# A fused attention and MLP layer on one core: semaphore waits that keep GpSimd's additions and some VectorE operations apart, three open rounds of sums, and a new written-out order

## The chip, the core and the metric

The kernel runs on one core of one Trainium2 chip. The core has a matrix engine (TensorE, PE in the profile), three engines for element-wise work (VectorE or DVE, ScalarE or ACT, GpSimd or POOL), a synchronization engine (SyncE, SP) and DMA queues that SP and GpSimd issue to. Each engine works through its own instruction stream in order and waits on semaphores where it needs another's result. The metric is the device time of one execution in microseconds. Three runs of the kernel before took 199.99 to 200.40, with a median of 200.25.

## The reference

One sequence of S = 2048 rows with D = 448 features in bf16. Two residual blocks follow each other, each behind a layer norm without weights:

```python
h  = x + A(layernorm(x)) ;  h2 = h + B(layernorm(h))

# A: 16 heads of 28; each position attends to itself and to 7 earlier ones, 2 apart
qkv = x @ wqkv
logits[s, w] = q[s] . k[s - 2*w] / sqrt(28)     for w = 0..7, masked where s - 2*w < 0
o = softmax_w(logits) @ v[s - 2*w] ;  return o @ wo

# B: a mixer and an MLP, F = 1792
h  = gelu(layernorm(x) @ w1)                    # 448 x 448
hs = concat(quarters of h, shifted by 1, -1, 2, -2 rows) @ w2
x1 = x + hs
return x1 + gelu(layernorm(x1) @ w3) @ w4       # 448 x 1792, 1792 x 448
```

## The kernel before

The rows are worked on in four tiles of 512 (t = 0 to 3), in 16 blocks of 128 partitions each. The phases of a tile are:

- `phase_N1`: statistics of the rows and the normalization `lntm`, then `doubled`, a small copy of the last 64 columns beside the others, so that pairs of matmuls can use half the rows each; `transposed` makes the transposed tile `actT`, either on TensorE (with the identity `ident`) or with a transposing DMA of the SP queue.
- `phase_A1` and `phase_V`: projections to queries, keys and values. ScalarE (and for some groups VectorE) takes the sums out of PSUM; for the values into `vt`, from where DMAs of GpSimd's queue put overlapping windows of 80 rows into `vw`.
- `phase_A2`: VectorE multiplies each query with its eight keys, `qk_r`, in four products per tile (128 x 4096, the last 128 x 2048); TensorE sums them over the heads' columns with the constant `zc`. Then the softmax: the largest logit `mx`, the difference `ls`, the exponential on ScalarE, the sum `zs`, its reciprocal, and the weights `pb`, all on VectorE but the exponential. TensorE transposes `pb`, ScalarE stores it in the `arena`.
- `phase_A3`: VectorE spreads the weights into a block diagonal `bd_r` (80 x 2048, four per tile), TensorE multiplies it with `vw`, ScalarE takes the result out as `actT`, TensorE multiplies with `wo_s` and adds the residual.
- `phase_B1`: the second layer norm and the matmuls with `w1`; ScalarE applies the GELU.
- `phase_B2`, `phase_W3`, `phase_B3`: these run on five units of 3, 4, 4, 4 and 1 blocks, since the row shifts of the mixer cross the tiles' borders. `phase_B2` multiplies with `w2_s` (the matmuls `w_s`, `arena`), VectorE adds the scaled residual (one `scalar_tensor_tensor` per block, `arena<-xin,rs_y,ps`), then comes a third layer norm. GpSimd adds the residual once more, in place: 16 additions `xb += xin` (`arena<-arena,xin`), one per block. `phase_W3` is the matmul with `w3` and its GELU into `h3T`, `phase_B3` the matmul with `w4`; VectorE scales and adds (`ost`), and SP's queue stores the result.

A layer norm's variance goes through VectorE (`rs_x`), then either GpSimd (`rs_y`, a power of -1/2) or ScalarE; `nm` is the negated mean. So at the places that matter the same stretch has VectorE's `rs_x`, `nm`, normalizations (`lntm`) and softmax beside GpSimd's power and additions.

The order is not made by a scheduler at run time. The phases first record operations with their tiles, readers and writers (`_Sched.group`). `schedule` then walks through `ORDER`, a written-out list of 1096 operation numbers, and hands each operation to its engine's stream in that order. On the way it gives out buffers (pools of PSUM banks, tiles of `lntm`, `actT`, `qk_r`, `bd_r` and others) and works out a modelled time for each operation, from which it derives some dependences between DMAs, the number of filler matmuls, and the order in which waits are listed. `_emit_plan` turns every dependence between two streams into a semaphore wait, unless an earlier wait implies it. So the modelled times change little but the order in the list changes each engine's stream. An operation flagged `block` is one that the model takes to run either on VectorE or on GpSimd at a time: the GpSimd additions on one side, and on the other the `qk_r` and `bd_r` products and most normalizations of VectorE. Before the change this is only a rule for the modelled times:

```python
if op.eng == "pool":
    waiting = op if blocked > st else None
    st = entry = max(st, blocked)
    if op.block: held = st + dur
elif op.block:
    ...                        # a waiting GpSimd operation is set back
    else: st = max(st, held)
    blocked = st + dur
```

The tile pool `P_win` has no memory behind it. `contract`, which makes the matmul groups of a projection, holds one of its tiles for each round of up to four groups: with one tile a second round cannot open in the list before the first has closed.

Nearly every instruction of the profile bears line 1090, `inst = getattr(eng, meth)(**kw)` in `emit_engine`, so instructions are told apart by their tiles.

Of the kernel before, what the change touches and what calls it, by code (L numbers as in the profile page):

```python
# [6 lines left out]
ALU = mybir.AluOpType  # L7
# [181 lines left out]
class _Sched:  # L189
# [69 lines left out]
    def schedule(self, dma_bw=240.0, dma_fixed=2000.0, table_load=1300.0):  # L259
# [18 lines left out]
        blocked = held = entry = 0.0; waiting = None  # L278
        assert sorted(ORDER) == list(range(n))
        for idx in ORDER:  # L280
# [45 lines left out]
            else:  # L326
# [3 lines left out]
                if op.eng == "pool":  # L330
                    waiting = op if blocked > st else None
                    st = entry = max(st, blocked)
                    if op.block:
                        held = st + dur
                elif op.block:
                    if waiting is not None and st <= entry + 50.0:
                        late = st + dur - entry
                        free["pool"] += late; waiting.t1 += late; entry += late
                        for ch in children[waiting.idx]:
                            if waiting in ch.deps:  # L340
                                rdy[ch.idx] = max(rdy[ch.idx], waiting.t1 - (self.OWN if ch.eng == "pool" else 0.0))
                        if waiting.block:
                            held += late
                    else:
                        st = max(st, held)
                    blocked = st + dur
# [67 lines left out]
def bass_sequential_preLN__sliding_local_dilated__mixer_s_mlp__prompt_kernel(  # L414
# [17 lines left out]
    EPS = 1e-5  # L432
# [15 lines left out]
    with ExitStack() as es:  # L448
# [41 lines left out]
        P_win = _Pool("win", None, 1)  # L490
# [39 lines left out]
        def dma(chan, out_ap, in_ap, nbytes, dur=450.0, eng="sp", behind=(), **kw):  # L530
            op = S.add(eng, "dma_start", dur, 1000.0 if eng == "pool" else 0.0 if not callable(chan) else -1300.0, chan=chan, nbytes=nbytes, out=out_ap, in_=in_ap, **kw)
            op.odeps.update(behind)
            return op
# [598 lines left out]
```

## Time and profile before

| | before |
|---|---|
| median of three runs | 200.25 us (199.99 to 200.40) |
| the profiled execution | 199.96 us |
| its span | 198.2 us |
| TensorE busy | 189.7 us, 96%, 1667 matmuls |
| VectorE busy | 121.7 us, 61%, 222 instructions |
| ScalarE busy | 143.4 us, 72%, 321 instructions |
| GpSimd busy | 46.0 us, 23%, 96 instructions |
| granted TensorE clock | 1.0 |

The profile shows one execution of the program, taken by the hardware's profiler. The span runs from its first to its last instruction. The slices cut the span into 40 equal parts of 4.95 us, and each digit is an engine's busy share in tenths (9 is 90% or more). The chain of waits follows the work that ended last back from the end: start, length, engine and instruction. A row of a timeline is a run of like instructions on one engine: the start (us), the length, engine, line, operation, tiles written and read, shape, count; a bracket at its end is the idle time just before it and what ended that. Rows can overlap by the depth of an engine's pipeline.

### The profile page before, as it was taken

What the parts mean: (1) busy time and instruction counts of PE and PEld (TensorE: products, weight loads), DVE (VectorE), ACT (ScalarE), POOL (GpSimd) and SP (SyncE); (2) the same over time, 40 slices, a digit from 0 to 9 for tenths busy, and PEclk for the clock granted to TensorE, in tenths of its full rate; (3) what the DMA queues carried; (4) which work ended last, traced back from release to release, by engine and by line L of the source; (5) the groups of instructions that cost most, each with busy time, mean ns of one, the idle gap of its engine ahead of it and who ended that gap; (6) DMA issues with size and microseconds to landing.
All of it is one profiled execution on the core that took longest, in us unless ns stands there. A gap on an engine that the chain in (4) does not pass through costs nothing.

```text
span 198.2 us, 4119 instructions
## 1 busy us (share of the span) xinstructions
PE 189.7 (96%) x1667; PEld 92.6 (47%) x1667; DVE 121.7 (61%) x222; ACT 143.4 (72%) x321; POOL 46.0 (23%) x96
## 2 busy tenths in 40 slices
PE   6899999889999989999989999999999999999994
PEld 2555333443454545544545444455444455446753
DVE  5888889999989999947957775101314052310024
ACT  4849986997999999997589699991345961645300
POOL 6540199003500000036040204302050000760000
PEclk9999999999999999999999999999999999999999
DMA  5950579943995000055410410009300023210003
GB/s 160 326 162 3 107 179 224 189 88 58 237 286 198 5 3 3 10 107 126 86 20 0 80 31 3 23 0 202 102 26 0 2 40 66 73 46 0 3 0 116
DMA packets 24467, 16.81 MB, mean 85 GB/s; under 512 B 17824, under 2 KB 22880, under 8 KB 24448
## 3 DMA queue, kind: packets, MB, share of 16 engines
q1 hardware_dynamic: 22368, 9.24, 19.7%
q0 software_dynamic: 2080, 7.31, 14.8%
q8 instruction: 13, 0.21, 0.4%
q14 instruction: 6, 0.05, 0.1%
HBM read 7.91 MB, written 1.84 MB: 49 GB/s over the span
## 4 chain that ended last, share of the span: by engine, by line
PE 62%; ACT 19%; DVE 8%; DMA 5%; POOL 4%; issue 1%; SPq 0%
PE ps L1090 62%; ACT arena L1090 5%; ACT actT L1090 5%; ACT vt L1090 3%; DMA vw<-vt 3%; ACT lntm L1090 2%; DVE qk_r L1090 2%; DMA xin<-in_A_x_dram 1%; DVE lntm L1090 1%; POOL w_s L1090 1%; POOL vw L1090 1%; DVE arena L1090 1%; ACT xin L1090 1%; POOL wo_s L1090 1%; ACT L1085 1%
## 5 line engine op out<-in xcount | busy, mean ns | idle before, releaser
L1090 PE MATMUL ps<-actT,arena 128*128 128x512 bf16 (+6 forms) x404 | 71.5, 344 | 0.3 <-ACT actT L1090 0.2
L1090 PEld LDWEIGHTS ps<-actT,arena 128*128 128x128 bf16 (+1 forms) x404 | 30.7, 97 | 37.4 <-issue 6.7
L1090 PE MATMUL ps<-arena,h3T 128*128 128x448 bf16 (+1 forms) x238 | 46.4, 342 | 0.0
L1090 ACT ACTIVATE h3T<-ps 128x512 bf16<-128x512 f32 (+1 forms) x60 | 30.6, 578 | 14.0 <-PE ps L1090 13.8
L1090 ACT ACTIVATE arena<-ps 128x512 bf16<-128x512 f32 (+5 forms) x64 | 32.0, 524 | 12.0 <-PE ps L1090 11.5
L1090 DVE SCALAR_TENSOR_TENSOR ost<-ps,mrs,arena 128x448 bf16<-128x448 f32 (+1 forms) x17 | 10.9, 654 | 37.8 <-PE ps L1090 35.7
L1090 DVE TENSOR_TENSOR qk_r<-arena 128x4096 bf16<-128x4096 bf16 (+1 forms) x16 | 31.8, 2016 | 2.8 <-PE ps L1090 2.8
L1090 PEld LDWEIGHTS ps<-arena,h3T 128*128 128x128 bf16 x238 | 22.6, 98 | 19.3 <-issue 0.5
L1090 POOL DMA_DIRECT2D vw<-vt x15 | 9.0, 605 | 48.9 <-DMA actT<-lntm 48.4
L1090 DVE TENSOR_TENSOR bd_r<-arena,bmask 80x2048 bf16<-80x2048 bf16 x16 | 18.7, 1214 | 2.2 <-ACT arena L1090 2.2
L1090 POOL TENSOR_TENSOR arena<-arena,xin 128x448 f32<-128x448 f32 x16 | 16.3, 1037 | 15.2 <-ACT lntm L1090 14.5
L1090 ACT ACTIVATE actT<-ps 128x512 bf16<-128x512 f32 (+2 forms) x27 | 17.8, 679 | 2.6 <-PE ps L1090 2.4
L1090 ACT ACTIVATE lntm<-arena,nm 128x448 bf16<-128x448 f32 x16 | 10.6, 662 | 8.6 <-DVE nm L1090 8.6
L1090 POOL TENSOR_TENSOR rs_y<-rs_x,mhalf 128x4 f32<-128x4 f32 (+1 forms) x5 | 4.7, 934 | 50.1 <-DVE rs_x L1090 50.1
L1090 PE MATMUL ps<-wo_s,actT 128*128 128x448 bf16 x64 | 14.5, 354 | 1.7 <-ACT actT L1090 1.6
L1090 DVE BATCH_NORM_STATS2 st<-xin 128x6 f32<-128x448 bf16 x24 | 13.8, 610 | 1.7 <-DMA xin<-in_A_x_dram 1.6
L1090 PE MATMUL ps<-actT,w_s 128*112 128x512 bf16 (+1 forms) x64 | 14.5, 387 | 0.0
L1090 DVE SCALAR_TENSOR_TENSOR arena<-xin,rs_y,ps 128x448 f32<-128x448 bf16 x16 | 10.4, 677 | 6.7 <-PE ps L1090 6.6
L1090 PE MATMUL ps<-w_s,arena 112*128 112x448 bf16 x64 | 13.6, 352 | 0.3 <-ACT arena L1090 0.3
L1090 PE MATMUL ps<-arena,actT 128*128 128x448 bf16 (+1 forms) x64 | 12.3, 353 | 0.5 <-ACT arena L1090 0.5
L1090 PEld LDWEIGHTS ps<-actT,w_s 128*112 128x112 bf16 (+1 forms) x64 | 6.5, 128 | 6.1 <-issue 2.0
L1090 PEld LDWEIGHTS ps<-w_s,arena 112*128 112x128 bf16 x64 | 6.0, 98 | 6.3 <-ACT arena L1090 1.1
(73 smaller groups left out, 190.4 us busy)
## 6 DMA issues: line engine op xcount, KB each, us to landing
out_dram<-ost SPq DMA_DIRECT2D x15, 112.0 KB, 1.7
arena<-in_B_w_dram POOLq DMA_DIRECT2D x1, 1568.0 KB, 15.2
arena<-in_B_w_dram POOLq DMA_DIRECT2D x1, 1344.0 KB, 10.4
vw<-vt POOLq DMA_DIRECT2D x4, 320.0 KB, 5.3
vw<-vt POOLq DMA_DIRECT2D x4, 256.0 KB, 5.2
xin<-in_A_x_dram SPq DMA_DIRECT2D x2, 448.0 KB, 5.8
xin<-in_A_x_dram SPq DMA_DIRECT2D x3, 224.0 KB, 5.0
arena<-in_A_wqkv_dram SPq DMA_DIRECT2D x1, 672.0 KB, 4.8
```

The lines of the kernel that those rows point to most:

```text
L1085: eng.preload_act_table_set("natural_log_exp_and_others")
L1090: inst = getattr(eng, meth)(**kw)
```

## The change

It has four parts. First, in `schedule` the flag `block` becomes a real wait: each flagged GpSimd operation now depends on the last flagged VectorE operation ahead of it in the list, and each flagged VectorE operation on the last flagged GpSimd one. Second, more of VectorE's operations get the flag: the small `nm` and `rs_x` operations and the `doubled` copies. Third, the pool `P_win` has three tiles instead of one. Fourth, two constants of the modelled DMA times are changed, and `ORDER` is another permutation of the same 1096 numbers.

```diff
 ORDER = [
-    0, 9, 8, 10, 1, 2, 3, 11, 6, 4, 35, 22, 36, 5, 37, 12, 23, 38, 13, 24, 14, 25, 39, 15, 26, 46, 16, 40, 27, 52, 17, 28, 41, 18, 53, 29, 47, 60,
...
+    0, 9, 10, 1, 2, 3, 11, 4, 35, 22, 36, 37, 12, 23, 38, 13, 24, 14, 25, 39, 15, 26, 46, 16, 40, 27, 17, 47, 28, 52, 41, 48, 18, 29, 53, 19, 30, 66,
...
-    def schedule(self, dma_bw=240.0, dma_fixed=2000.0, table_load=1300.0):
+    def schedule(self, dma_bw=215.0, dma_fixed=2000.0, table_load=1300.0):
...
-        blocked = held = entry = 0.0; waiting = None
+        blocked = entry = 0.0; waiting = None; guard = dict(dve=None, pool=None)
...
                 if op.eng == "pool":
-                    waiting = op if blocked > st else None
-                    st = entry = max(st, blocked)
                     if op.block:
-                        held = st + dur
+                        waiting = None
+                        if guard["dve"]:
+                            op.deps.add(guard["dve"]); st = max(st, guard["dve"].t1)
+                        guard["pool"] = op
+                    else:
+                        waiting = op if blocked > st else None
+                        st = entry = max(st, blocked)
                 elif op.block:
+                    if guard["pool"]:
+                        op.deps.add(guard["pool"]); st = max(st, guard["pool"].t1)
+                    guard["dve"] = op
                     if waiting is not None and st <= entry + 50.0:
...
-                        if waiting.block:
-                            held += late
-                    else:
-                        st = max(st, held)
                     blocked = st + dur
...
-        P_win = _Pool("win", None, 1)
+        P_win = _Pool("win", None, 3)
...
-            op = S.add(eng, "dma_start", dur, 1000.0 if eng == "pool" else ...
+            op = S.add(eng, "dma_start", dur + 100.0 * (eng == "pool"), 1000.0 if eng == "pool" else ...
...
-            dve("tensor_scalar", 4, ns=78.0, out=nm[:, kind, lo:lo + m], ...
+            dve("tensor_scalar", 4, ns=78.0, block=True, out=nm[:, kind, lo:lo + m], ...
...
-                dve("tensor_scalar", 4, ns=78.0, out=rs_x[:, kind, 0, i:i + m], in0=var, scalar1=by, scalar2=EPS, op0=ALU.mult, op1=ALU.add)
+                dve("tensor_scalar", 4, ns=78.0, block=True, out=rs_x[:, kind, 0, i:i + m], in0=var, scalar1=by, scalar2=EPS, op0=ALU.mult, op1=ALU.add)
...
-            dve("tensor_copy", 64, ns=142.0, out=ln(lambda v: v[:, lo:lo + n, D:512]), ...
+            dve("tensor_copy", 64, ns=142.0, block=True, out=ln(lambda v: v[:, lo:lo + n, D:512]), ...
```

The flagged `tensor_scalar` operations shown stand for all of them: every `nm` and every `rs_x` operation of VectorE has the flag after the change. The program has the same operations on the same engines: 1668 matmuls instead of 1667, one more of the filler matmuls that TensorE runs while it waits for the first tile.

More of the change, by code (lines that the diff above doesn't have):

```diff
@@ L530, in dma @@
         def dma(chan, out_ap, in_ap, nbytes, dur=450.0, eng="sp", behind=(), **kw):
-            op = S.add(eng, "dma_start", dur, 1000.0 if eng == "pool" else 0.0 if not callable(chan) else -1300.0, chan=chan, nbytes=nbytes, out=out_ap, in_=in_ap, **kw)
+            op = S.add(eng, "dma_start", dur + 100.0 * (eng == "pool"), 1000.0 if eng == "pool" else 0.0 if not callable(chan) else -1300.0, chan=chan, nbytes=nbytes, out=out_ap, in_=in_ap, **kw)
             op.odeps.update(behind)
@@ L596, in sums_stats @@
             lo, m = tiles[0], len(tiles)
-            dve("tensor_scalar", 4, ns=78.0, out=nm[:, kind, lo:lo + m], in0=mv[:, kind, lo:lo + m, 0], scalar1=-1.0 / D, scalar2=None, op0=ALU.mult)
+            dve("tensor_scalar", 4, ns=78.0, block=True, out=nm[:, kind, lo:lo + m], in0=mv[:, kind, lo:lo + m, 0], scalar1=-1.0 / D, scalar2=None, op0=ALU.mult)
             for n, i in enumerate(tiles):
@@ L619, in rstd @@
                 if not summed and (norm == "a" or kind == 1):
-                    dve("tensor_scalar", 4, ns=78.0, out=nm[:, kind, i:i + m], in0=mv[:, kind, i:i + m, 0], scalar1=-1.0, scalar2=None, op0=ALU.mult)
+                    dve("tensor_scalar", 4, ns=78.0, block=True, out=nm[:, kind, i:i + m], in0=mv[:, kind, i:i + m, 0], scalar1=-1.0, scalar2=None, op0=ALU.mult)
                 power_act(first)
@@ L629, in rstd @@
             if not summed and (norm == "a" or kind == 1):
-                dve("tensor_scalar", 4, ns=78.0, out=nm[:, kind, i:i + m], in0=mv[:, kind, i:i + m, 0], scalar1=-1.0, scalar2=None, op0=ALU.mult)
+                dve("tensor_scalar", 4, ns=78.0, block=True, out=nm[:, kind, i:i + m], in0=mv[:, kind, i:i + m, 0], scalar1=-1.0, scalar2=None, op0=ALU.mult)
             if kind == 1:
-                dve("tensor_scalar", 4, ns=78.0, out=rs_x[:, kind, 1, i:i + m], in0=var, scalar1=by * (1.0 + EPS), scalar2=EPS * EPS,
+                dve("tensor_scalar", 4, ns=78.0, block=True, out=rs_x[:, kind, 1, i:i + m], in0=var, scalar1=by * (1.0 + EPS), scalar2=EPS * EPS,
                     op0=ALU.mult, op1=ALU.add)
@@ L635, in rstd @@
             elif summed:
-                dve("tensor_scalar", 4, ns=78.0, out=rs_x[:, kind, 0, i:i + m], in0=var, scalar1=by, scalar2=EPS, op0=ALU.mult, op1=ALU.add)
+                dve("tensor_scalar", 4, ns=78.0, block=True, out=rs_x[:, kind, 0, i:i + m], in0=var, scalar1=by, scalar2=EPS, op0=ALU.mult, op1=ALU.add)
             else:
-                dve("tensor_scalar", 4, ns=78.0, out=rs_x[:, kind, 0, i:i + m], in0=var, scalar1=EPS, scalar2=None, op0=ALU.add)
+                dve("tensor_scalar", 4, ns=78.0, block=True, out=rs_x[:, kind, 0, i:i + m], in0=var, scalar1=EPS, scalar2=None, op0=ALU.add)
             if kind == 1:
@@ L641, in rstd @@
                     shifts(1)
-                dve("tensor_scalar", 4, ns=78.0, out=rs_x[:, kind, 0, i:i + m], in0=var, scalar1=by, scalar2=EPS, op0=ALU.mult, op1=ALU.add)
+                dve("tensor_scalar", 4, ns=78.0, block=True, out=rs_x[:, kind, 0, i:i + m], in0=var, scalar1=by, scalar2=EPS, op0=ALU.mult, op1=ALU.add)
             power(0)
@@ L674, in doubled @@
         def doubled(ln, lo, n):
-            dve("tensor_copy", 64, ns=142.0, out=ln(lambda v: v[:, lo:lo + n, D:512]), in_=ln(lambda v: v[:, lo:lo + n, 384:D]))
+            dve("tensor_copy", 64, ns=142.0, block=True, out=ln(lambda v: v[:, lo:lo + n, D:512]), in_=ln(lambda v: v[:, lo:lo + n, 384:D]))
         def transposed(ln, how, n=4, w=2):
```

74 rows, old and new, of the table ORDER are left out of this document.

## The prediction

> **What bounds the kernel now.** I read the page's totals and slices first, then the chain of waits, then the timeline of each engine around every wait of TensorE.
>
> ```profile
> span 198.2 us, 4119 instructions
> PE 189.7 (96%) x1667; PEld 92.6 (47%) x1667; DVE 121.7 (61%) x222; ACT 143.4 (72%) x321; POOL 46.0 (23%) x96
> ...
> PE   6899999889999989999989999999999999999994
> ...
> DVE  5888889999989999947957775101314052310024
> ACT  4849986997999999997589699991345961645300
> ```
>
> The reader is to see two halves. In slices 7 to 17 (35 to 85 us) VectorE and ScalarE are at 9 tenths beside TensorE; from slice 21 on TensorE alone is full. The chain says the same:
>
> ```profile
> 87.94 3.43 DVE qk_r L1090 x2
> ...
> 92.62 1.11 DVE lntm L1090
> 93.73 0.91 DVE nm L1090
> ...
> 101.71 93.95 PE ps L1090 x664
> ```
>
> From 101.71 us to the end TensorE runs 664 matmuls without a wait. Nothing that another engine does there pays, unless it makes TensorE wait. So a gain has to come from TensorE's idle time before 101.71, which the timeline of TensorE gives:
>
> ```profile
> 6.77 0.40 PE L1090 MATMUL ps<-ident,lntm 128*128 128x128 bf16 x4 [0.70 <-DVE lntm L1090]
> ...
> 37.34 1.79 PE L1090 MATMUL ps<-arena,actT 64*128 64x448 bf16 x10 [0.52 <-ACT arena L1090]
> ...
> 41.63 0.93 PE L1090 MATMUL ps<-wo_s,actT 128*128 128x448 bf16 x4 [0.86 <-ACT actT L1090]
> ...
> 44.75 0.93 PE L1090 MATMUL ps<-wo_s,actT 128*128 128x448 bf16 x4 [0.26 <-ACT actT L1090]
> ...
> 64.49 2.44 PE L1090 MATMUL ps<-w_s,arena 112*128 112x448 bf16 x12 [0.34 <-ACT arena L1090]
> ...
> 73.97 0.93 PE L1090 MATMUL ps<-wo_s,actT 128*128 128x448 bf16 x4 [0.45 <-ACT actT L1090]
> ...
> 78.65 4.50 PE L1090 MATMUL ps<-actT,arena 128*128 128x384 bf16 x28 [0.20 <-ACT actT L1090]
> ...
> 91.81 1.05 PE L1090 MATMUL ps<-qk_r,zc 128*32 128x512 bf16 x16
> ...
> 97.54 3.38 PE L1090 MATMUL ps<-arena,h3T 128*128 128x448 bf16 x17
> 101.71 0.64 PE L1090 MATMUL ps<-ident,pb 128*80 128x128 bf16 x8 [0.79 <-DVE pb L1090]
> ```
>
> Six waits on ScalarE between 37 and 79 us make 0.52 + 0.86 + 0.26 + 0.34 + 0.45 + 0.20 = 2.63 us, and one on VectorE at 101.71 makes 0.79 us. All of them together are 3.42 us, the most that a new order can win.
>
> **The wait at 101.71, where the change acts.** The timelines of GpSimd and VectorE show what made `pb` late:
>
> ```profile
> 91.53 1.05 POOL L1090 TENSOR_TENSOR rs_y<-rs_x,mhalf 128x4 f32<-128x4 f32 x1 [1.80 <-DVE rs_x L1090]
> 92.57 2.05 POOL L1090 TENSOR_TENSOR arena<-arena,xin 128x448 f32<-128x448 f32 x2
> ...
> 91.28 0.16 DVE L1090 TENSOR_SCALAR rs_x<-mv 128x4 f32<-128x4 f32 x1
> 92.62 1.11 DVE L1090 TENSOR_SCALAR lntm<-xin,nm,rs_y 128x448 bf16<-128x448 bf16 x1 [1.17 <-POOL rs_y L1090]
> 93.65 0.99 DVE L1090 TENSOR_SCALAR nm<-mv 128x4 f32<-128x4 f32 x1
> 94.56 1.00 DVE L1090 TENSOR_SCALAR lntm<-xin,nm,rs_y 128x448 bf16<-128x448 bf16 x3
> 95.60 0.23 DVE L1090 COPY lntm<-lntm 128x256 bf16<-128x256 bf16 x1
> 95.74 0.68 DVE L1090 TENSOR_REDUCE mx<-ps 128x64 f32<-128x512 f32 x1
> 96.46 0.69 DVE L1090 TENSOR_TENSOR ls<-ps,mx 128x512 f32<-128x512 f32 x1
> 97.06 0.67 DVE L1090 SCALAR_TENSOR_TENSOR arena<-xin,rs_y,ps 128x448 f32<-128x448 bf16 x1
> ...
> 100.96 0.69 DVE L1090 TENSOR_TENSOR pb<-ls,zs 128x512 bf16<-128x512 f32 x1
> ...
> 103.97 1.25 DVE L1090 TENSOR_TENSOR bd_r<-arena,bmask 80x2048 bf16<-80x2048 bf16 x1 [2.24 <-ACT arena L1090]
> ```
>
> While the two additions run (92.57 to 94.62) VectorE gets through two instructions. Three normalizations behind them take 1.00, 0.33 each, so from 92.62 to 94.56 about 1.5 us are lost to the additions.
>
> [...]
>
> In the changed program, the built order on each engine is: on GpSimd one addition, then the power `rs_y`, both after `rs_x`; on VectorE `rs_x`, `mx`, `nm` (waits for that addition), `ls`, four normalizations, the copy, then the four residual operations, `zs`, the reciprocal and `pb`. By rows: `rs_x` ends at 91.44; the addition (half of 2.05) ends about 92.5, the power (1.05) about 93.6. `mx` needs the 16 sums that end at 91.81 + 1.05 = 92.86, so it runs from 92.9, `nm` finds its addition done, and `ls` starts about 93.7 and lets go at 94.3 (0.60, from 96.46 to 97.06). The power is done by then. Four normalizations are 1.33, the copy 0.14: 95.8. From the first residual operation to the end of `pb` it is 101.65 - 97.06 = 4.59, with the same operations in between, so `pb` ends at 100.4 instead of 101.65. TensorE's last matmul before it ends at 97.54 + 3.38 = 100.92. The 0.79 goes whole, with 0.5 us to spare. Bounds: from 0 to -0.79; I take -0.79, since the margin is worked out from rows of this very stretch.
>
> What is late next: VectorE's `bd_r` products now wait for GpSimd's 46th update, the power and two additions after the next `rs_x`, which is put just ahead of `pb` (about 99.7): 99.7 + 1.05 + 2.05 = 102.8. They started at 103.97 and had waited 2.24 for ScalarE, so 1.2 us of cover are left; without it, the first TensorE reader of `bd_r` is several microseconds further on. The other guard waits (for `ost`, `nm`, the last copy) lie in the part where TensorE runs without a break; I cost them at nothing, bar the last, which is a rival below.
>
> **The new order before 90 us.** These are its parts on VectorE and ScalarE:
>
> ```profile
> 1.06 0.81 DVE L1090 MEMSET wo_s<- 128x896 uint32 x1 [1.06 <-PEq L1117]
> 1.87 0.27 DVE L1090 MEMSET vt<- 128x256 uint32 x1
> ...
> 8.23 1.15 DVE L1090 BATCH_NORM_STATS2 st<-xin 128x6 f32<-128x448 bf16 x2 [0.51 <-DMA xin<-in_A_x_dram]
> ...
> 87.94 3.43 DVE L1090 TENSOR_TENSOR qk_r<-arena 128x4096 bf16<-128x4096 bf16 x2 [2.47 <-PE ps L1090]
> ...
> L1090 ACT ACTIVATE vt<-ps 128x448 bf16<-128x448 f32 x16 | 8.4, 552 | 0.0
> ```
>
> The first copy stands one normalization later (0.33 by the row above), and TensorE waits for it at 6.77. Cost 0 to +0.33; I take 0, because TensorE meets ScalarE again at 37.34 with 0.52 idle. One extra filler matmul falls into the idle 0.70 before 6.77: nothing.
>
> Two memsets, 0.81 + 0.27 = 1.08, move from the start, where VectorE waited for the first load, to behind the first four tiles. There VectorE was idle 0.51 for a load, so it comes up to 0.57 later into its full stretch. The third query product also waits for sums that TensorE now issues behind three more matmuls, up to 0.6 (0.2 each, 3.38 for 17 in the row at 97.54). Cost to TensorE 0 to +1.2; I take 0: VectorE stands idle 2.47 at 87.94, waiting for TensorE, which covers a VectorE that is late by itself.
>
> The last value projection's evictions are moved ahead of the first GELU's table load: one more of 0.55 before the `w_s` matmuls of 64.49, and one fewer before those of 73.97. Three of the matmuls of another tile stand between the `bd_r` ones ahead of 41.63, whose wait of 0.86 they can fill. Bounds for all six waits on ScalarE: from -2.63 to +0.55. I take 0, nearest to what both full engines allow: what TensorE saves at 41.63, it finds again as a VectorE or ScalarE that is not ready at the next place.
>
> GpSimd's queue issues the `vw` and weight loads in another sequence, but the same ones, and the transposing load at 40 us no longer waits for the `vw` load that stood last. No bracket in TensorE's timeline names those loads before 90 us: 0. The planner's constants (bandwidth, GpSimd's issue) and the three `win` tiles do nothing on the chip except through the order.
>
> Sum: -0.79 + 0 + 0 = -0.8 us. The profiled execution took 199.96 for a span of 198.19; it becomes 199.2. It lies 0.29 under the median of 200.25, so the median becomes 199.4.
>
> **The rivals.**
>
> *The order wins more.* If half of the 2.63 us of waits on ScalarE go as well, 200.25 - 0.79 - 1.3 = 198.2. For it: the matmuls put ahead of 41.63, and rounds of sums that may interleave. Against: the 9s of ScalarE and VectorE in slices 7 to 17.
>
> *The wait comes back.* The `w_s` matmuls behind 101.71 need the transposing load of the tile whose copy ended at 95.83.
>
> ```profile
> actT<-lntm SPq DMA_TRANSPOSE x8, 4.4
> ```
>
> That copy stays where it is (95.8), the load lands 4.4 later at 100.2, and TensorE would come for it at 101.4. If the load takes 1.2 us more, or `pb` loses the 0.5 of its margin and more, TensorE stands again, for up to 0.79: 199.4 to 200.25, and taken at 200.1, since a load that misses its time by more than its cover mostly gives the whole stall back. Against: the cover of 1.2.
>
> *Slower: VectorE's full stretch starts later and TensorE follows.* The place is 8 to 79 us. Price: 0.57 + 0.6 = 1.2 on VectorE, and 0.55 on ScalarE ahead of the GELU. If TensorE's start of W3 (78.65) is later by more than 1.2, the 0.79 no longer pays for it and the kernel is slower by over 0.4; with the whole price, 200.25 - 0.79 + 1.75 = 201.2, and with the first copy's 0.33 on top 201.5. For it: slices 7 to 17 have hardly a gap. Against: the idle 2.47 and the idle of 2.63.
>
> A smaller danger sits in the tail:
>
> ```profile
> 170.21 0.18 DVE L1090 COPY lntm<-lntm 128x64 bf16<-128x64 bf16 x1
> ...
> 177.31 0.39 PE L1090 MATMUL ps<-ident,lntm 128*128 128x128 bf16 x4
> ```
>
> The copy for the last tile ended 6.9 us before TensorE came for it; now it waits for three additions (3.1, at 2.05 for two) and sits behind `ost` operations. By the additions alone 3.8 are left, so I cost it at nothing; if that cover is gone, TensorE stands there by what is missing, and this belongs to the slower share.
>
> **How the numbers follow.** The forecast 0.42 (199.4, its own range 198.8 to 199.8); the order wins more 0.10 (198.2); the wait comes back 0.15 (200.1); slower 0.33 (200.7 to 201.5). 0.2% is 0.4 us, about what a measurement of this kernel can tell from no change. Faster is the first two, 0.52; same 0.15; slower 0.33. The range reaches over all four: 198.1 to 201.5.
>
> **What would show it.** Right: TensorE's row for `pb` carries no bracket; VectorE's normalizations behind the power take 0.4 each; `nm` takes 0.17; W3 starts within 0.5 us of 78.65. Wrong: brackets between 37 and 79 us that sum to more than 3.4; a VectorE with slices under 8 tenths between 35 and 85; a new bracket behind 101 us that names VectorE or GpSimd.

## The result, and the profile after

The changed kernel takes 199.41 us in the median of 22 runs (198.42 to 201.59), the kernel before 200.01 in 22 runs beside it (199.67 to 201.60). The ratio is 0.9967, with a 95% interval of 0.9952 to 0.9982. The forecast was 199.4. Here and below the ratios and their intervals are taken over the undisturbed executions and are no quotients of the medians, which are taken over all, so the two can differ by some 0.2%.

The profiled execution took 199.71 us for a span of 197.9. Its totals and slices, from the page:

```profile
span 197.9 us, 4122 instructions
PE 190.2 (96%) x1668; PEld 93.4 (47%) x1668; DVE 120.2 (61%) x222; ACT 143.3 (72%) x321; POOL 48.0 (24%) x96
...
PE   6999999879999889999999999999999999999994
...
DVE  3998989998999999767946777000343043230024
```

Counted from 0, TensorE's slice 20 (99 to 104 us) was an 8 and is a 9; slice 8 (40 to 45 us) was an 8 and is a 7. VectorE's slice 16 (79 to 84 us) was a 9 and is a 7. The timelines of VectorE and GpSimd around `pb` in the changed kernel:

```profile
88.63 3.43 DVE L1093 TENSOR_TENSOR qk_r<-arena 128x4096 bf16<-128x4096 bf16 x2 [1.74 <-PE ps L1093]
92.00 0.17 DVE L1093 TENSOR_SCALAR rs_x<-mv 128x4 f32<-128x4 f32 x1
93.42 0.69 DVE L1093 TENSOR_REDUCE mx<-ps 128x64 f32<-128x512 f32 x1 [1.25 <-PE ps L1093]
94.03 0.16 DVE L1093 TENSOR_SCALAR nm<-mv 128x4 f32<-128x4 f32 x1
...
94.75 1.31 DVE L1093 TENSOR_SCALAR lntm<-xin,nm,rs_y 128x448 bf16<-128x448 bf16 x4
...
100.14 0.69 DVE L1093 TENSOR_TENSOR pb<-ls,zs 128x512 bf16<-128x512 f32 x1
103.73 3.49 DVE L1093 TENSOR_TENSOR bd_r<-arena,bmask 80x2048 bf16<-80x2048 bf16 x3 [2.90 <-POOL arena L1093]
```

```profile
92.25 1.04 POOL L1093 TENSOR_TENSOR arena<-arena,xin 128x448 f32<-128x448 f32 x1 [1.27 <-DVE rs_x L1093]
93.25 1.05 POOL L1093 TENSOR_TENSOR rs_y<-rs_x,mhalf 128x4 f32<-128x4 f32 x1
100.22 1.49 POOL L1093 TENSOR_TENSOR rs_y<-rs_x,mhalf 128x4 f32<-128x4 f32 x1 [5.92 <-DVE rs_x L1093]
101.69 2.01 POOL L1093 TENSOR_TENSOR arena<-arena,xin 128x448 f32<-128x448 f32 x2
```

The addition now runs while VectorE waits for TensorE's sums anyway; four normalizations take 1.31, 0.33 each, and `nm` 0.16. TensorE's timeline on the same stretch and its waits before 80 us:

```profile
37.59 1.23 PE L1093 MATMUL ps<-arena,actT 64*128 64x448 bf16 x7 [0.67 <-ACT arena L1093]
40.01 0.42 PE L1093 MATMUL ps<-bd_r,vw 80*32 80x64 bf16 x32 [0.22 <-issue]
...
42.41 0.93 PE L1093 MATMUL ps<-wo_s,actT 128*128 128x448 bf16 x4 [0.86 <-ACT actT L1093]
...
65.08 1.69 PE L1093 MATMUL ps<-w_s,arena 112*128 112x448 bf16 x8 [0.62 <-ACT arena L1093]
69.86 0.42 PE L1093 MATMUL ps<-ident,pb 128*80 128x128 bf16 x4 [0.19 <-ACT actT L1093]
71.88 0.93 PE L1093 MATMUL ps<-wo_s,actT 128*128 128x448 bf16 x4 [0.44 <-ACT actT L1093]
75.03 0.93 PE L1093 MATMUL ps<-wo_s,actT 128*128 128x448 bf16 x4 [0.45 <-ACT actT L1093]
...
92.32 1.05 PE L1093 MATMUL ps<-qk_r,zc 128*32 128x512 bf16 x16
...
98.20 3.38 PE L1093 MATMUL ps<-arena,h3T 128*128 128x448 bf16 x17
101.42 0.61 PE L1093 MATMUL ps<-ident,pb 128*80 128x128 bf16 x8
```

`pb` has no bracket. But the last sums of products start at 92.32 where they started at 91.81, so in this execution TensorE comes 0.51 later to the stretch, and the waits between 37 and 80 us sum to 3.45 where they summed to 2.63. From here on one measure is useful: TensorE's own work from the start of these sums to `pb` is 101.42 - 92.32 = 9.10 us. VectorE's way from the same start to the end of `pb` was 101.65 - 91.81 = 9.84 before and is 100.83 - 92.32 = 8.51. So the stretch went from 0.74 too long to 0.59 of margin. TensorE's start on `pb` moved from 9.90 to 9.10 behind the start of the sums, and 0.8 us are won there; in this execution 0.51 of it had been lost ahead.

### The profile page after: what moved, and what is told of

The parts are those of the page before. It is cut to its first block, busy times and chain, and to the rows that moved or that the text cites. A ratio compares the mean times of both kernels' runs of the same rounds, so it can differ in the third digit from the quotient of the medians.

```text
span 197.9 us, 4122 instructions
## 1 busy us (share of the span) xinstructions
PE 190.2 (96%) x1668; PEld 93.4 (47%) x1668; DVE 120.2 (61%) x222; ACT 143.3 (72%) x321; POOL 48.0 (24%) x96
## 4 chain that ended last, share of the span: by engine, by line
PE 68%; ACT 21%; POOL 4%; DMA 3%; issue 1%; DVE 1%; POOLq 0%; ACTq 0%
PE ps L1093 68%; ACT arena L1093 6%; ACT lntm L1093 4%; ACT vt L1093 4%; DMA vw<-vt 3%; ACT actT L1093 3%; POOL vw L1093 2%; POOL w_s L1093 1%; POOL wo_s L1093 1%; ACT xin L1093 1%; ACT L1088 1%; ACT L1093 1%; ACT ls L1093 1%; ACT nmr L1093 0%; ACT rs_x L1093 0%
## 5 line engine op out<-in xcount | busy, mean ns | idle before, releaser
L1093 PE MATMUL ps<-actT,arena 128*128 128x512 bf16 (+6 forms) x404 | 72.7, 344 | 0.0
L1093 PE MATMUL ps<-arena,h3T 128*128 128x448 bf16 (+1 forms) x238 | 48.0, 342 | 0.0
L1093 ACT ACTIVATE arena<-ps 128x512 bf16<-128x512 f32 (+4 forms) x64 | 31.5, 526 | 9.8 <-PE ps L1093 9.0
L1093 PE MATMUL ps<-arena,actT 128*128 128x448 bf16 (+1 forms) x64 | 12.8, 354 | 0.7 <-ACT arena L1093 0.7
L1093 DVE COPY lntm<-lntm 128x256 bf16<-128x256 bf16 (+2 forms) x16 | 3.3, 208 | 14.5 <-ACT lntm L1093 12.4
L1093 ACT ACTIVATE vt<-ps 128x448 bf16<-128x448 f32 x16 | 8.4, 554 | 1.8 <-DMA vw<-vt 1.8
```

## The experiments

OLD and NEW are the two lists. Where a kernel mixes them, the list is cut behind operation 550, VectorE's last query product (88 to 92 us); the two parts ahead of it differ by two operations on either side. Each line of times has the kernel before from the same chip beside it.

**The new list behind the cut alone.**

```diff
-ORDER = NEW
+ORDER = OLD[:OLD.index(550) + 1] + [x for x in NEW if x not in OLD[:OLD.index(550) + 1]]
```

> The changed kernel with the list of before up to VectorE's last query product (88 to 92 us), and the new list, with its waits, behind it. Theory 'two parts': the new list behind the cut is worth the stall of 0.79 us at pb and the new list ahead of it costs some 0.5 (in the two profiles TensorE comes 0.50 us later to the last sums of products, 92.32 against 91.81, and starts on pb 0.29 earlier, 101.42 against 101.71). Then this kernel is at 200.0 - 0.8 to 0.95 = 199.05 to 199.2, below the changed kernel's 199.4. Theory 'late part only': the new list ahead of the cut costs nothing in the median, and the 0.5 is one execution's: then it is at 199.4, as the changed kernel. pb's row on TensorE carries no bracket in both.

Measured: 199.30 us (12 runs), before 200.09; ratio 0.9968 (0.9945 to 0.9991). `pb` has no bracket; from the sums to its end it is 100.32 - 91.81 = 8.51. The late part alone is the gain, 0.8 in the medians. The median lies between the forecasts of the two theories; the ratio is that of the whole change (0.9967), which speaks for "late part only", but with an interval of 0.2% to either side the times alone don't decide it.

**The new list ahead of the cut alone,** the list of before behind it, without the added waits (both `op.deps.add(guard[...])` taken out, as in the next experiment).

```diff
-ORDER = NEW
+ORDER = NEW[:NEW.index(550) + 1] + [x for x in OLD if x not in NEW[:NEW.index(550) + 1]]
```

> The reverse: the new list up to VectorE's last query product, the list of before behind it, without the added waits. Theory 'two parts': 200.0 + 0.5 = 200.5 or, since a later TensorE waits less for pb, 200.0 to 200.5, with pb's bracket between 0.3 and 0.8. Theory 'late part only': 200.0, with a bracket of 0.8.

Measured: 199.86 us (12 runs), before 200.09; ratio 0.9995 (0.9976 to 1.0014): no difference. From the sums to the end of `pb` it is 101.45 - 91.60 = 9.85 as before. The bracket of 0.8 isn't there by name, since the planner put four filler matmuls into the gap it saw; TensorE still starts on `pb` only at 101.51.

**The new list throughout, without the added waits.**

```diff
                         if guard["dve"]:
-                            op.deps.add(guard["dve"]); st = max(st, guard["dve"].t1)
+                            st = max(st, guard["dve"].t1)
...
                     if guard["pool"]:
-                        op.deps.add(guard["pool"]); st = max(st, guard["pool"].t1)
+                        st = max(st, guard["pool"].t1)
```

> The changed kernel without the added waits: same list, same instructions on each engine in the same sequence, but the GpSimd additions no longer wait for VectorE nor VectorE for them. Theory 'the order does it': the first addition starts some 1.2 us sooner, at 91.0, beside the query product, and pb keeps its 0.5 us of margin: 199.4, within 0.2. Rival 'the waits do it': the addition and the query product hold each other up by up to the length of the addition (1.04 us), the last sums come that much later, and pb is late by up to 0.8: 199.7 to 200.2, with a product behind 88 us that takes over 2.2 us instead of 2.06 mean.

Measured: 200.32 us (12 runs), before 200.09; ratio 0.9998 (0.9978 to 1.0019). The gain is gone. The timelines of GpSimd, VectorE and TensorE show where:

```profile
90.99 1.02 POOL L1093 TENSOR_TENSOR arena<-arena,xin 128x448 f32<-128x448 f32 x1
```

```profile
88.68 4.42 DVE L1093 TENSOR_TENSOR qk_r<-arena 128x4096 bf16<-128x4096 bf16 x2 [1.74 <-PE ps L1093]
```

```profile
93.15 1.05 PE L1093 MATMUL ps<-qk_r,zc 128*32 128x512 bf16 x16 [0.72 <-DVE qk_r L1093]
```

The addition starts 1.26 us sooner, at 90.99, and the two query products take 4.42 instead of 3.43: 0.99 more, for an addition of 1.02. The way from the sums to `pb` is 8.52, as good as with the waits, but the sums start 0.72 late. The rival "the waits do it" holds here, with the very product that it named; the median lies 0.1 above its range.

**The waits, flags and open rounds with the list of before.**

```diff
-ORDER = NEW
+ORDER = OLD
```

> The changed kernel with the list of before throughout: the added waits, the flags and the three open rounds alone. In the list the two additions stand behind normalizations, so that by the waits VectorE runs four normalizations at 0.33 first, and the copy waits for one addition, the next nm for the second. Theory 'the order does it': the waits move the lost time from the normalizations to the copy and to nm, and pb stays late: 199.8 to 200.2, pb's bracket 0.5 to 0.9. Rival 'the waits do it': pb's bracket under 0.3, 199.3 to 199.6.

Measured: 199.96 us (12 runs), before 200.09; ratio 0.9996 (0.9977 to 1.0015): no difference. Its profile is that of its slowest execution, 201.59 us, so only the distances within the stretch are read from it. The timelines of VectorE, GpSimd and TensorE:

```profile
94.76 1.00 DVE L1093 TENSOR_SCALAR lntm<-xin,nm,rs_y 128x448 bf16<-128x448 bf16 x3
96.91 0.23 DVE L1093 COPY lntm<-lntm 128x256 bf16<-128x256 bf16 x1 [1.15 <-POOL arena L1093]
```

```profile
95.84 1.03 POOL L1093 TENSOR_TENSOR arena<-arena,xin 128x448 f32<-128x448 f32 x1 [1.50 <-DVE lntm L1093]
```

```profile
93.58 1.05 PE L1093 MATMUL ps<-qk_r,zc 128*32 128x512 bf16 x16
...
102.52 1.03 PE L1093 MATMUL ps<-ident 128*128 128x512 bf16 x4
103.38 0.61 PE L1093 MATMUL ps<-ident,pb 128*80 128x128 bf16 x8
```

The normalizations are quick (0.40 for the first, 1.00 for the other three), and the copy then waits 1.15 us for the addition. From the sums to the end of `pb` it is 102.97 - 93.58 = 9.39: 0.45 less than before, but TensorE is through with its own work 8.94 behind the start of the sums. Here too the planner has put four fillers into the gap, from 102.52 to 103.38, so that TensorE starts on `pb` only 0.41 after its end, where it took 0.06 before. So waits alone put the copy's wait of 1.15 in the place of the longer normalizations and take off a part of the delay, and in this kernel the fillers use most of that part up (TensorE starts on `pb` 9.80 behind the start of the sums, before 9.90). What the waits alone would gain without these fillers, no run shows; an estimate from these rows is 0.4 us at most. As built, they gain nothing without the new list, and the new list gains nothing without them.

**Two additions moved, in the kernel before.** No added wait; operations 416 and 418 are taken out of OLD and put behind 529, the next power.

```diff
-    ..., 527, ..., 416, ..., 418, ..., 529, ..., 417, ...
+    ..., 527, ..., 529, 416, 418, ..., 417, ...
```

> The kernel before, with its own list and no added wait; only the two GpSimd additions of 92.57 to 94.62 are moved behind the next power (to about 102.8, ahead of the third). Theory 'those two additions make pb late': the normalization and nm behind the power take 0.36 and 0.17 again instead of 1.11 and 0.99, pb ends some 1.6 us earlier at about 100.1, TensorE's row for pb (which comes at 100.9) has no bracket of 0.79: 200.05 - 0.8 = 199.25. Rival 'something else that the new list moves does it' (the power behind one addition, the sums ahead of the normalizations): the bracket stays above 0.5 and the time within 0.3 of 200.05. A third outcome is that the bracket goes and the time stays, because three additions now run beside the bd_r products at 103 to 106.

Measured: 199.16 us (10 runs, 198.76 to 199.35), before 200.01; ratio 0.9947 (0.9927 to 0.9967). Moving two operations of 1096 gives the whole gain of the change (0.9967); the intervals don't tell the two apart. The timelines of VectorE, GpSimd and TensorE:

```profile
92.98 0.40 DVE L1090 TENSOR_SCALAR lntm<-xin,nm,rs_y 128x448 bf16<-128x448 bf16 x1 [1.18 <-POOL rs_y L1090]
93.29 0.16 DVE L1090 TENSOR_SCALAR nm<-mv 128x4 f32<-128x4 f32 x1
...
103.21 5.04 DVE L1090 TENSOR_TENSOR bd_r<-arena,bmask 80x2048 bf16<-80x2048 bf16 x3 [2.24 <-ACT arena L1090]
```

```profile
102.04 4.00 POOL L1090 TENSOR_TENSOR arena<-arena,xin 128x448 f32<-128x448 f32 x3
```

```profile
92.17 1.05 PE L1090 MATMUL ps<-qk_r,zc 128*32 128x512 bf16 x16
...
101.12 0.61 PE L1090 MATMUL ps<-ident,pb 128*80 128x128 bf16 x8
```

The normalization and `nm` are back at 0.40 and 0.16 (they were 1.11 and 0.99), and TensorE's row for `pb` has no bracket. From the sums to the end of `pb` it is 100.89 - 92.17 = 8.72, so VectorE's way is 1.12 shorter and not the 1.6 expected. The collision isn't gone, it is moved: three `bd_r` products take 5.04 where they take 3.49 in the changed kernel, and three additions 4.00 where two take 2.01. There it costs nothing: TensorE comes for the first of the three products at 107.76 and finds it done.

**One added wait alone**: the first addition, behind `rs_x`.

```diff
                         if guard["dve"]:
-                            op.deps.add(guard["dve"]); st = max(st, guard["dve"].t1)
+                            if guard["pool"] is None:
+                                op.deps.add(guard["dve"])
+                            st = max(st, guard["dve"].t1)
```

(the wait of VectorE for GpSimd is out as above)

> The changed kernel with one of its added waits alone: the first GpSimd addition waits for rs_x behind the last query product. All other added waits are gone. Theory 'one collision decides': 199.4 within 0.2, the query products at 88 to 92 take 3.43 for two. Rival 'the later waits count as well' (additions beside bd_r, ost and the last copy): 199.7 to 200.3, as without any of them.

Measured: 199.52 us (12 runs), before 200.01; ratio 0.9953 (0.9926 to 0.9981). The two query products take 3.43 again. One of the added waits does what all do, within what the runs can tell; without the wait of `bd_r` these products start 11.28 us behind the sums (103.15 - 91.87) instead of 11.41, which moves nothing at the end.

**One filler less, and shorter fillers**, in the changed kernel.

```diff
-                if self.filler is not None and order["pe"]:
+                if self.filler is not None and len(order["pe"]) > 13:
```

```diff
-                mm(b(), ident[:], bass.AP(ident, 0, [[128, 128], [0, 4], [1, 128]]), n == 0, n == WARM - 1, 512)
+                r = 4 if n < 10 else 1
+                mm(b(lambda v, r=r: v[:, 0:128 * r]), ident[:], bass.AP(ident, 0, [[128, 128], [0, r], [1, 128]]), n == 0, n == WARM - 1, 128 * r)
```

> The changed kernel without the one filler matmul that it has more ahead of the first transposition; all else the same. In the profiles so far the fillers start 0.43 us apart until a step between 4.5 and 7.3 us from the start, 0.21 apart behind it, and the first transposition comes at 6.77 to 7.48. Theory 'the fillers set the first transposition': where the step is late it comes up to 0.43 earlier, where it is early nothing changes: 199.1 to 199.3 in the median, and fewer runs above 199.8. Rival 'the load sets it': 199.4.

> The changed kernel without the additional filler, and with the last three of the other thirteen at a quarter of their length (128 columns), so that TensorE is through with them by about 6.2 us even at the slow pace. Theory 'the fillers set the first transposition': it starts within 0.1 us of the copy's end (6.7 to 6.8) in each execution: 198.9 to 199.2. Rival 'the step needs the work': with TensorE idle ahead of the first transposition the step to the fast pace comes later, the matmuls behind it run at 0.43 for 512 columns, and the time is 199.4 to 200.

Measured: 199.27 and 199.47 us (12 runs each), before 200.01; ratios 0.9956 (0.9935 to 0.9978) and 0.9961 (0.9937 to 0.9985). Neither differs from the changed kernel (0.9967) by more than the intervals; what the filler costs is not settled. The second median lies in the range of the rival "the step needs the work", but its profile doesn't show what that rival names: two full fillers behind the first transposition take 0.59 us there as elsewhere. What makes the filler hard to measure is the fillers' pace, in TensorE's timelines of two kernels with thirteen of them (the kernel with the moved additions, and the one with one filler less):

```profile
1.59 5.73 PE L1090 MATMUL ps<-ident 128*128 128x512 bf16 x13 [1.59 <-POOL epsilon L1090]
```

```profile
1.59 4.70 PE L1093 MATMUL ps<-ident 128*128 128x512 bf16 x13 [1.59 <-POOL epsilon L1093]
6.99 0.40 PE L1093 MATMUL ps<-ident,lntm 128*128 128x128 bf16 x4 [0.69 <-DVE lntm L1093]
```

Thirteen took 4.47 before, 4.70 and 5.73 here. In every trace they start 0.43 us apart up to some moment between 4.5 and 7.5 us, and where fillers are left behind it they start 0.21 to 0.22 apart; the moment differs from execution to execution. In the kernel before the starts are 0.43 apart up to 4.55 and 0.22 from 4.82 on, in the changed kernel 0.43 up to 6.26 and 0.21 to 0.22 from 6.68 on. The mean granted clock of this stretch is 1.00 all the same (the third value from the end, in the windows of the changed kernel):

```profile
0.00:7.20 7.20, 5.61 (x16) 2.07 (x17) 4.12 (x15) 3.70 (x11) 3.65 (x22) 1.00 0.70 216
```

What makes the pace step up, and what moves the moment, no run shows.

**The changed kernel again, and a mix.** The second has NEW ahead of the cut, OLD with the moved additions behind it, no added wait and one filler less.

```diff
-ORDER = NEW
+ORDER = NEW[:NEW.index(550) + 1] + [x for x in OLD_ADDS_LATER if x not in NEW[:NEW.index(550) + 1]]
```

> The changed kernel once more, for a second profile and for a comparison on the same chip: 199.4 within 0.2 by all theories. What the profile tells apart is why TensorE came 0.5 us later to the sums at 92.32 in the first one. If the new list costs that, it is there again (92.2 to 92.4); if it is the moment at which the fillers' pace steps up and the landing of the transposing load, it moves with those two, between 91.6 and 92.6.

> The new list up to the last query product, the list of before behind it with the two additions moved behind the next power, no added wait, and one filler less ahead of the first transposition. Theory 'the move of two additions is the whole gain, and the new list ahead of the cut costs nothing': 199.0 to 199.3, as the kernel before with the two additions moved (199.16). Theory 'the new list ahead of the cut is a gain of its own' (its profile came 0.2 us earlier to the sums at 91.6): 198.8 to 199.0. If it costs something: above 199.4.

Measured: 199.42 us (9 runs) and 199.35 us (12 runs, from 198.40 to 201.57), before 200.12; ratios 0.9965 (0.9951 to 0.9980) and 0.9961 (0.9937 to 0.9985). In the two profiles the last sums start at 92.63 and at 91.59: one list ahead of the cut, and 1.0 us between them. Only part of it lies in the fillers' pace (the first transposition starts at 7.38 and 6.85). ScalarE's timeline of the changed kernel, of its repetition and of the mix, at the `vt` of the third tile:

```profile
40.45 1.42 ACT L1093 ACTIVATE vt<-ps 128x448 bf16<-128x448 f32 x3 [1.82 <-DMA vw<-vt]
```

```profile
40.86 1.42 ACT L1093 ACTIVATE vt<-ps 128x448 bf16<-128x448 f32 x3 [1.95 <-DMA vw<-vt]
```

```profile
39.34 1.42 ACT L1093 ACTIVATE vt<-ps 128x448 bf16<-128x448 f32 x3 [0.96 <-DMA vw<-vt]
```

ScalarE may overwrite a `vt` buffer only when the `vw` loads that read it have landed. In the kernel before they land in time: its ScalarE has no such wait (the list of before with the added waits has one of 0.31, in the execution of 201.59). Both lists have the loads of the first tile behind the same eight weight loads in GpSimd's queue, before as the 10th to 13th load and in the new list as the 11th to 14th, behind one more of the second tile. And the first load of the queue is now one that needs the second tile's `vt`, where in OLD a `wo` load went first: the queue starts at 25.26 instead of 23.71, and the last load that ScalarE needs is issued at 33.51 instead of 31.86. The first `wo_s` matmuls start 1.96 us behind this `vt` in all three: 42.41, 42.82, 41.30. The chain of waits of the changed kernel says the same:

```profile
28.49 2.69 POOL w_s L1093 x4
31.18 2.33 POOL vw L1093 x4
33.51 6.92 DMA vw<-vt
40.45 1.42 ACT vt L1093 x3
...
42.41 2.53 PE ps L1093 x42
```

**The `vw` loads ahead of the weights**, in the changed kernel and in the mix. The list moves four operations, and the `vw` loads (`vwa` shown, `vwb`, `vwc` and `vwp` likewise) need no longer stand behind the weights in it:

```diff
-    ..., 95, ..., 291, ..., 96, ..., 103, ..., 292, ..., 198, ..., 199, ..., 289, ..., 200, ...
+    ..., 95, ..., 198, 199, 200, 289, 291, ..., 96, ..., 103, ..., 292, ...
...
-            dma("vwa%d" % sl, ..., 600.0, "pool", behind=rest[t:])
+            dma("vwa%d" % sl, ..., 600.0, "pool", behind=())
```

> The changed kernel with the four vw loads of the first tile ahead of the weight loads in GpSimd's queue, all else the same. In all eight profiles with the new list ahead of 88 us ScalarE stands 0.96 to 1.95 us (in the four where it is longest 1.62 to 1.95) at the vt of the third tile, and in each TensorE starts on wo_s 1.99 us after the landing of the last of these loads (39.31 to 40.84). Theory 'the new queue sequence makes a wait of its own': the wait for vw is gone, the first wo_s starts at 40.4 to 41.5 instead of 42.41 and 42.82, and of that 0.5 to 1.0 stays: 198.5 to 199.0. Rival 'ScalarE and VectorE are full there, and the time is found again': the bracket moves on to a later place before 79 us, and it is 199.2 to 199.5.

> The same move of the loads, and one filler less, in the kernel that has the new list up to the last query product, the list of before behind it, and the two additions behind the next power, without an added wait (199.35). Theory 'the queue sequence makes a wait': 198.5 to 199.0. Rival 'found again': 199.2 to 199.4.

Measured: 198.75 us (6 runs, 198.39 to 198.91) and 198.59 us (6 runs, 198.36 to 198.86), before 200.32; ratios 0.9913 (0.9884 to 0.9942) and 0.9909 (0.9882 to 0.9935). Both beat the changed kernel: their intervals end below its own (0.9952 to 0.9982), and each of their runs is below 198.92, where two of its 22 are. ScalarE's and TensorE's timelines of the first:

```profile
38.68 1.40 ACT L1093 ACTIVATE vt<-ps 128x448 bf16<-128x448 f32 x3
```

```profile
41.16 0.93 PE L1093 MATMUL ps<-wo_s,actT 128*128 128x448 bf16 x4
...
46.36 1.05 PE L1093 MATMUL ps<-qk_r,zc 128*32 128x512 bf16 x16 [0.34 <-DVE qk_r L1093]
...
91.46 1.05 PE L1093 MATMUL ps<-qk_r,zc 128*32 128x512 bf16 x16
```

The wait is gone, `wo_s` starts at 41.16 without a bracket, a part comes back as 0.34 at the next products, and the last sums start at 91.46, 0.86 earlier than in the changed kernel, although this execution's first transposition was the later one (7.27 against 7.11). Counted from the first transposition to the last sums, which leaves the fillers' pace out, it is 84.19 and 84.39 us with the loads ahead, 84.63 to 85.26 in the other kernels with the new list ahead of the cut (85.69 without the waits, where the sums start 0.72 late), and 84.93 to 85.05 with the list of before (86.10 in the execution of 201.59). The theory "a wait of its own" holds. Whether the same move would pay with the list of before, no run shows.

## Why the prediction was right, point by point

- **The number**: 199.4 against 199.41 is closer than the working deserves. The forecast takes 0.79 off a base of 200.25, the median of three runs; in 22 runs the kernel before is at 200.01, and the gain is 0.60 in the medians and 0.66 by the ratio (0.36 to 0.96 by its interval). A base that was 0.24 too high and a gain that was some 0.2 too large cancel, and that is luck.
- **The stall at `pb` goes whole** (-0.79): right. No bracket; VectorE's way became 1.33 us shorter, forecast 1.25; the margin is 0.59, forecast 0.5. The runs with one part of the lists and with two moved additions put its price at 0.79 to 0.85 in the median.
- **The cause, two additions beside the normalizations**: shown by the kernel that moves them alone. The 1.5 us lost to them were real: the start of the first normalization and that of the other three lie 1.94 apart in the kernel before and 0.38 with the additions moved. (`nm` alone takes 0.16; beside the additions it took 0.99.)
- **The waits and the list, each alone**: with the list of before the waits gain nothing in the time (0.9996), though there VectorE's way became 0.45 shorter and four fillers took the place. These fillers also go against the step by which the planner's constants do nothing on the chip except through the order: with the order of before, the changed planner gives that kernel 1672 matmuls instead of 1667. Which part of its model does so, no run separates. Without its waits the new list gains nothing either (0.9998), since its addition stands so early that it starts beside the last query product, at 90.99. The wait that matters is the one behind `rs_x`.
- **VectorE beside an addition**: the new list without waits shows the loss once more, at another place. An addition of 1.02 makes two query products 0.99 longer (4.42 instead of 3.43), and takes no longer itself (1.04 behind the wait). What holds VectorE up there, no run shows.
- **What is late next, `bd_r`**: they waited for GpSimd until 103.73, 0.9 later than worked out: the power started at 100.22, 0.5 later, and took 1.49 instead of 1.05. It cost nothing, as said; TensorE came at 108.63.
- **The order before 90 us, taken at 0**: about right in the sum, by two errors. Its own signs of being wrong came: the waits between 37 and 80 us, 2.63 before, were to stay under 3.4 and are 3.45, VectorE has a slice under 8 ahead of 85 us (slice 16, a 7), and the matmuls with `w3` start at 79.44, not within 0.5 of 78.65. (Already before, not all of slices 7 to 17 is full: ScalarE's slice 9 is a 7, VectorE's slice 17 a 4.) The step that failed is GpSimd's queue: "No bracket in TensorE's timeline names those loads before 90 us: 0". TensorE's brackets name ScalarE, and it is ScalarE that stands 0.96 to 1.95 us for them. The chain of waits of the kernel before has these loads on it, shortly ahead of ScalarE's `vt` at 39.30; the prediction read that chain only from 87.94 on:

```profile
30.07 1.79 POOL vw L1090 x3
31.86 6.44 DMA vw<-vt
```

  Against this loss stands a gain inside the same part: with the loads ahead, `wo_s` starts without the 0.86. The three matmuls put between the `bd_r` ones fit it, but no run takes them out alone. "The order wins more" was thus there to be had, and was spent on the loads: moving them ahead wins 1.57 us in the medians instead of 0.60, each against the kernel before beside it.
- **The other terms at nothing**: the tail showed no new bracket. Idle time for the extra filler is left in one of the eight profiles with fourteen fillers only (0.83 in the kernel with one added wait); in the others the fillers run longer than the load. Its price is below what the medians tell.

## What to carry to other kernels

Where one engine's work gets longer beside another's, as the two products here (4.42 us instead of 3.43), look to the list first, since here the waits alone gained nothing: put the second engine's work where the first one waits anyway, and then pin it there with one semaphore, or move it to a stretch whose reader is far off. When a list is reordered, walk every engine's waits, not only the bound's: a load that lands in time for the bound may be late for the engine that feeds it, and what it frees (a buffer to be overwritten) counts as much as what it brings. And look at what the planner puts into a gap: fillers that cover an expected wait keep the engine when the wait becomes shorter.

## What was not expected

- A 0.99 us longer pair of products and a whole gain hang on when one addition of 1.02 us starts.
- Additions beside VectorE's work cost 0.8 us at 92 us and nothing at 103, though at 103 both sides lose: 1.55 us on VectorE and, at 1.0 for each addition alone, 1.0 on GpSimd.
- TensorE's first matmuls change their pace at a moment that moves over some 2.9 us between executions, while the granted clock shows 1.0.
